# Squared scores of the first batch: columns 1 and 2 get three groups by DMA transpose in place of matmuls

## The chip, the cores and the metric

The kernel runs on one core of a Trainium2 chip. The metric is the device time of one execution in microseconds, as the median of the runs shown. Engines are called by the profile's names: PE is TensorE, DVE VectorE, ACT ScalarE, POOL GpSimd, SP SyncE.

## What is computed

Eight sequences (batches) of 3008 tokens go through a gated attention without softmax, and the result through a two-layer block. The scores are z times its own transpose, so the matrix of squared scores is symmetric, and that is what this case turns on.

```python
def _attn_ref(u, v, z):                      # u, v: (8, 3008, 256); z: (8, 3008, 64)
    scores = (1.0 / S) * np.matmul(z, z.transpose(0, 2, 1))
    attn = np.maximum(scores, 0.0) ** 2
    return u * np.matmul(attn, v)

def _moe_ref(x, w_in, w_out):                # w_in: (256, 2048), w_out: (2048, 256)
    h = x @ w_in
    return (h * np.cos(h)) @ w_out
```

## The kernel before

The 3008 tokens are 24 blocks of 128 (the last is a half), and four blocks make a group of 512. So the matrix of squared scores of a batch is 6 x 6 groups. A column c holds 512 queries, and a row R holds 512 keys; group (c,R) is a tile of 128 x 2048 half-precision numbers in one of 18 slots. Tiles that were computed have the key `a`, tiles that were turned have the key `t`.

**How a group comes about.** It is computed in two halves, called visits of pairs (`s_visit`). `s_matmuls` (L271) makes scores by matmuls that use 64 rows of the array, into four banks of PSUM. `s_squares` takes the positive part into `rt`, on ACT (L307) or, for one bank in four of the first columns, on DVE (L305), and squares it into the slot on DVE (L309). Both half visits of a first-batch group follow each other, so a group shows as four matmuls of L271. A group below the diagonal (R < c) is the transpose of group (R,c) above it. In most of the kernel it is not computed: `turn_s` (L321) issues a DMA transpose on SP from the computed slot to another one. A group on the diagonal, from column 4 of the first batch on, is computed as a triangle and filled by small transposes (L288, L293, L296).

**The first columns are an exception.** `direct(b, c, R)` is true for columns 0 to 2 of batch 0: there all six groups of a column are computed, below the diagonal too. The table `TURNS` has planned times for the transposes of the first batch; `None` means that the group is not turned.

**How a column is used.** `av_chunk` and `av_bank` (L362) multiply each block of the column with its block of v and sum in two banks (`ps_acc`). In columns 0 to 2 that is 46 products, in eight parts of up to six, with the rows in the order c, c+1, ..., so the groups below the diagonal come last. `moving` picks the tile: the computed one if there is one, otherwise the turned one. The last half block is added by `av_half` (L339). `finish` (L389) multiplies the two banks by the turned u (`ut`) and frees them; the next column's products need them. From column 4 on, part of the product is done with fewer multiplications: DVE forms sums and differences of tiles (`a_sums1` L439 and L441, `a_sums2` L451) and of v (`v_sums` L409 to L412), and PE multiplies them (`product`, L482).

**The two-layer block.** `h_quantum` makes h (L516), its cosine on ACT (L520) and the product on DVE (L523). `y_quantum` (L533) multiplies by w_out; ACT copies the result (L540). Score banks, h banks and y banks share the pool `ps_w` of six.

**What sets the order.** Each piece of work has a planned time in units, of which a column has eight; pieces are emitted in order of time, and every engine then runs its own instructions in order. PE's order is pinned. POOL issues all loads of v, u, z and the weights (L121), each held back until PE has reached a given matmul. SP issues all transposes, one after another: turned z (`turn_z`, L144), turned u (`turn_u`, L181, one `ut` for each column, from the buffers `ust0` and `ust1` in turn), groups (L321) and triangles (L296). Slots are given out ahead by `place`, from planned lifetimes (`use`): a tile goes into the slot that has been free longest. If the tile before is still being read, the writer waits.

In the profile the columns 0, 1, 2 of the first batch end near 25, 39 and 57 us, and column 3 near 81 us.

Of the kernel before, what the change touches and what calls it, by code (L numbers as in the profile page):

```python
# [14 lines left out]
def kernel(  # L15
# [31 lines left out]
    U = 8  # L47
# [184 lines left out]
    fresh = {}  # L232
    turned = {}

    def direct(b, c, R):


        return b == 0 and c <= 2

    def triangle(b, c, R):  # L240

# [2 lines left out]
    halves = {}  # L244
    slot_of = {}

    TURNS = {(0, 0, 1): None, (0, 0, 2): None, (0, 1, 2): None,
             (0, 0, 3): 1.0, (0, 0, 4): 2.4, (0, 1, 3): 7.8, (0, 0, 5): 8.0,
             (0, 2, 3): 14.4, (0, 1, 4): 14.6, (0, 2, 4): 15.8, (0, 1, 5): 20.0,
             (0, 2, 5): 22.0}  # L250
# [4 lines left out]
    def seven(b, c):  # L255

        return [] if (b, c) <= (0, NC // 2) else WSET[c]
# [20 lines left out]
    def s_squares(b, c, R, p, banks):  # L278
# [32 lines left out]
        if direct(b, c, R):  # L311
            behind(ins)
        if p == 1:
            fresh[(b, c, R)] = [t[:, :, k, :] for k in range(K)]
            if R > c and (b, c, R) not in TURNS:
                turn_s(b, c, R)

    def turn_s(b, c, R):
        tt = slot("t", b, c, R)
        turned[(b, c, R)] = tt  # L320
        nc.sync.dma_start_transpose(  # L321
            tt.rearrange("p s k w -> p (s k) w"),
            halves[(b, c, R)].rearrange("p s k w -> p (s k w)"))
# [10 lines left out]
    def av_half(b, c):  # L334

        a = fresh[(b, c, NC - 1)][K - 1]
        for nh in range(NDH):
            h = slice(nh * JLAST, (nh + 1) * JLAST)
            chain(nc.tensor.matmul(  # L339
                accs[(b, c)][nh],  # L340
                vs(b, NG - 1)[h, G - 1, nh * P:(nh + 1) * P],
                a[h], start=False, stop=False, skip_group_check=True))

    def wide(b, c):
        return min(CW, S - c * CW)

    def moving(b, c, j):
        R, k = divmod(j, K)
        if (b, c, R) in fresh:
            return CW, fresh[(b, c, R)][k]  # L350
        w = wide(b, c)
        tt = turned[(b, R, c)].rearrange("p s k w -> p s (k w)")
        return w, tt[:, k, 0:w]
# [48 lines left out]
    def v_sums(b, R):  # L402

        j = R * K
        t = vs(b, j // G)[:, j % G:j % G + K, :].rearrange("p (h k) d -> p h k d", h=2)
        o = vsum[R]
        b12, b22 = t[:, :, :, P:2 * P], t[:, 1, :, P:2 * P]
        left = t[:, 0, :, :].rearrange("p k (d w) -> p d k w", w=P)
        after(nc.vector.tensor_tensor(o[:, 0:3:2], b12, left, ALU.subtract).ins,  # L409
              before[-1], NOSYNC)  # L410
        nc.vector.tensor_tensor(o[:, 1], b22, o[:, 0], ALU.subtract)
        nc.vector.tensor_tensor(o[:, 3], t[:, 1, :, 0:P], o[:, 1], ALU.subtract)  # L412
# [24 lines left out]
    def a_sums1(b, c, R):  # L437
        s1 = quarters(b, c, R, (0, 1))
        after(nc.vector.tensor_tensor(s1, s1, quarters(b, c, R, (1, 1)), ALU.add).ins,  # L439
              before[-1], NOSYNC)  # L440
        nc.vector.tensor_tensor(  # L441
            second(b, c, R), s1, quarters(b, c, R, (0, 0)), ALU.subtract)
# [109 lines left out]
    def at(t, rank, f):  # L552
        events.append((t, rank, len(events), f))
# [9 lines left out]
    scores = []  # L563
    when = {}
    for b in range(B):
        pairs = [(b, c, R, p) for c, R in groups for p in range(2)]
        for i in range(0, len(pairs), NV):
            some = [pr for pr in pairs[i:i + NV] if not direct(*pr[:3])]
            t = b * span - lead + span * i / len(pairs)
            if some:  # L570
                scores.append((2 * math.floor(t / 2) + 1.2, some))
        for c in range(NC):
            if direct(b, c, c):
                for i in range(NC):
                    R = (c + i) % NC
                    scores.append((c * U + 4 * i / 3 - 3.1, [(b, c, R, 0), (b, c, R, 1)]))
    for t, some in scores:
        for pr in some:
            when[pr[:3]] = max(t, when.get(pr[:3], t))
# [3 lines left out]
    def use(key, first, last):  # L583
        a, z = lives.get(key, (first, last))
        lives[key] = (min(a, first), max(z, last))
# [10 lines left out]
    for t, some in scores:  # L596
        for b, c, R, p in some:
            use(("a", b, c, R), t, t + 1)
            if p == 1 and R > c and TURNS.get((b, c, R), t) is not None:
                t = TURNS.get((b, c, R), t)  # L600
                use(("t", b, c, R), t + 0.8, t + 2.5)
                use(("a", b, c, R), t, t + 3)
    for b in range(B):
        for R in range(NW):
            at(b * span + (TSUM[R] if b else 3 * U + 1 + 1.5 * R), 2, lambda b=b, R=R: v_sums(b, R))
        for c in range(NC):
            t = b * span + c * U
            W = seven(b, c)
            d = direct(b, c, c)
            ready = 1.5 + when[(b, c, NC - 1)]  # L610
            first, last = (0.6, 6.93) if d else (HALF[c] if W else 1.0, 7.3)
            room = [i for i, sc in enumerate(scores)
                    if max(ready, t + first) < sc[0] < t + last and i not in also]
            if room:
                also[min(room, key=lambda i: scores[i][0])] = lambda b=b, c=c: av_half(b, c)
            else:
                at(t + last, 3, lambda b=b, c=c: av_half(b, c))
            if d or not W:
                order = [(c + i) % NC for i in range(NC)]
            else:  # L620
                order = [R for R in range(NC) if R not in W]
            blocks = [R * K + k for R in order for k in range(K) if R * K + k < NJ - 1]
            if d:
                places = [(t + q + (0.5 if q < U - 1 else -0.05), 3) for q in range(U)]
            elif W:
                for i, R in enumerate(W):
                    at(t + SUM1[c][0] + SUM1[c][1] * i, 2, lambda b=b, c=c, R=R: a_sums1(b, c, R))
                    use(("x", b, c), t + SUM1[c][0], t + XEND)
                    use(("t", b, R, c) if R < c else ("a", b, c, R), t, t + 6.5)
                    at(t + SUM2[c][0] + SUM2[c][1] * i, 2.5, lambda b=b, c=c, R=R: a_sums2(b, c, R))  # L630
                at(t + WADD[c], 2.6, lambda b=b, c=c: keep(b, c, 0))
                at(t + RADD[c], 2.6, lambda b=b, c=c: keep(b, c, 8))
                done = [0, 0]
                for o, what in PLAN[c]:
                    for piece in what.split():
                        if piece[0] == "P":
                            n = int(piece[1])
                            at(t + o, 2, lambda b=b, c=c, n=n: product(b, c, n))
                            if n in (1, 5, 6, 7):
                                at(t + o + 0.02, 2.1, lambda b=b, c=c, n=n: keep(b, c, n))  # L640
                            continue
                        nh, size = "AB".index(piece[0]), int(piece[1:])
                        part = blocks[done[nh]:done[nh] + size]
                        done[nh] += size
                        end = done[nh] >= len(blocks)
                        at(t + o, 2, lambda b=b, c=c, nh=nh, part=part, end=end:
                           av_bank(b, c, nh, part, False, end))
                        for j in part:
                            R = j // K
                            use(("a", b, c, R) if R >= c else ("t", b, R, c), t + o, t + o + 0.3)  # L650
                assert done == [len(blocks)] * 2, (done, len(blocks))
                at(t + 7.45, 2, lambda b=b, c=c: finish(b, c))
                places = []
            else:
                places = [(t + q // 2 * 2 + (1.4 if q % 2 else 1.0), (4, 2)[q % 2])
                          for q in range(U)]
            n = 0
            for o, size in places:
                part = blocks[n:n + size]
                if part:  # L660
                    first, end = n == 0 and not W, n + size >= len(blocks)
                    at(o, 2, lambda b=b, c=c, part=part, first=first, end=end:
                       av_chunk(b, c, part, first, end))
                    for j in part:
                        R = j // K
                        use(("a", b, c, R) if R >= c or d else ("t", b, R, c), o, o + 0.3)
                n += size
            use(("a", b, c, NC - 1), t, t + last)
    place()
# [2 lines left out]
    for m in range(NT):  # L672
        b, i = divmod((m + 1) * TW - 1, S)
# [3 lines left out]
        for ts in range(NTS):  # L677
            for f4 in range(NFT // FG):
                at(th + U + 2 * ts + 0.1 + 0.2 * f4, 4,
                   lambda m=m, ts=ts, f4=f4: y_quantum(m, ts, f4))  # L680
    for key, t in TURNS.items():
        if t is not None:
            at(t, 3.5, lambda key=key: turn_s(*key))
    for b in range(B):
        t = b * span
# [73 lines left out]
```

## Time and profile before

| | |
|---|---|
| Median of 3 runs | 1214.15 us (1213.55 to 1215.6) |
| Profiled execution | 1214.96 us, span 1212.8 us |
| PE busy | 1206.3 us (99%), 8421 matmuls |
| DVE busy | 1020.1 us (84%) |
| ACT busy | 831.8 us (69%) |
| POOL busy | 145.8 us (12%) |
| SP's transposes (queue q1) | 356448 packets, 88.73 MB |
| POOL's loads (queue q0) | 100400 packets, 29.77 MB |

The page cuts the span into 40 slices of 30.3 us, with the busy share of an engine in tenths. A timeline has start and duration in us, engine, line, operation, the tiles written and read and how many instructions were merged; the brackets hold the idle time before the first of them and what ended it. For a DMA the timeline's duration is that of the issue by its queue, and the landing is told apart. Times in the text are us from the span's start.

### The profile page before, as it was taken

Reading aid. Unit: us, or ns where it says so; the run is one execution under the profiler, and the core shown is the slowest. Engines: PE = TensorE matmul, PEld = TensorE weight load, DVE = VectorE, ACT = ScalarE, POOL = GpSimd, SP = SyncE. Lnnn points to the kernel's source line nnn. Section 1 sums busy time; section 2 is a strip of 40 time slices with the busy share of each in tenths; the row PEclk is TensorE's granted clock in tenths of the full one; section 3 lists DMA queues with packets and bytes.
Section 4 is the critical chain, followed back from the end, with each engine's and each line's share of the span. In section 5 each row is a group of like instructions: output and inputs, shape, how many; then the busy total and the mean of one; then the engine's idle time right before and its main releaser. Section 6 shows DMA issues by size and latency. Waiting matters only on the chain.

```text
span 1212.8 us, 22944 instructions
## 1 busy us (share of the span) xinstructions
PE 1206.3 (99%) x8421; PEld 766.7 (63%) x8421; DVE 1020.1 (84%) x1995; ACT 831.8 (69%) x1741; POOL 145.8 (12%) x201
## 2 busy tenths in 40 slices
PE   9999999999999999999999999999999999999998
PEld 3356666666666666666666666666666666666666
DVE  7888988888888888888888888888888888888875
ACT  6767767677676777767777677776776767767555
POOL 3210101001010010100101011011110111100000
PEclk9999999999999999999999999999999999999999
DMA  9997968679586795857968579596695857956411
GB/s 147 186 168 132 148 92 131 111 120 154 103 112 113 120 155 102 129 104 113 155 103 133 101 112 161 96 133 104 109 162 94 133 104 112 159 94 120 73 33 48
DMA packets 484225, 145.02 MB, mean 120 GB/s; under 512 B 432400, under 2 KB 484112, under 8 KB 484112
## 3 DMA queue, kind: packets, MB, share of 16 engines
q1 hardware_dynamic: 356448, 88.73, 45.1%
q0 software_dynamic: 100400, 29.77, 24.9%
q10 hardware_dynamic: 27264, 25.06, 6.4%
q8 instruction: 66, 1.08, 0.4%
q14 instruction: 47, 0.39, 0.1%
HBM read 60.29 MB, written 24.64 MB: 70 GB/s over the span
## 4 chain that ended last, share of the span: by engine, by line
PE 97%; DMA 1%; issue 0%; DVE 0%; ACT 0%; POOL 0%; ACTq 0%; POOLq 0%; DVEq 0%
PE w L533 27%; PE w L516 26%; PE acc L482 19%; PE acc L362 18%; PE w L271 6%; PE acc L339 1%; DMA w_out<-in_moe_w_out_dram 1%; PE w L716 0%; ACT rt L307 0%; DVE s L309 0%; POOL zst L121 0%; PE w L222 0%; DVE x L389 0%; ACT zT L227 0%; DVE rt L305 0%
## 5 line engine op out<-in xcount | busy, mean ns | idle before, releaser
L520 ACT ACTIVATE c<-w 128x512 f16<-128x512 f32 x752 | 436.9, 619 | 258.7 <-PE w L516 210.8
L523 DVE TENSOR_TENSOR g<-w,c 128x512 f16<-128x512 f32 x752 | 492.3, 683 | 61.2 <-ACT c L520 59.5
L533 PE MATMUL w<-w_out,g 128*128 128x256 f16 x3008 | 448.6, 273 | 0.1
L516 PE MATMUL w<-x,w_in 128*128 128x512 f16 x1504 | 445.7, 379 | 0.0
L533 PEld LDWEIGHTS <-g 128*128 128x128 f16 x3008 | 294.1, 98 | 191.7 <-issue 0.8
L362 PE MATMUL acc<-s,v 128*128 128x512 f16 (+1 forms) x1024 | 290.6, 378 | 0.1
L307 ACT ACTIVATE rt<-w 128x512 f16<-128x512 f32 x489 | 253.1, 613 | 43.9 <-PE w L271 43.9
L309 DVE TENSOR_TENSOR s<-rt 128x1024 f16<-128x1024 f16 x254 | 172.7, 688 | 85.9 <-ACT rt L307 84.7
L516 PEld LDWEIGHTS <-w_in 128*128 128x128 f16 x1504 | 146.9, 98 | 73.3 <-issue 3.5
L482 PE MATMUL acc<-s,vsum 128*128 128x256 f16 (+1 forms) x1184 | 154.7, 270 | 0.0
L121 POOL DMA_DIRECT2D ust<-in_u_dram x112 | 81.2, 730 | 559.6 <-PE acc L362 534.9
L362 PEld LDWEIGHTS <-v 128*128 128x128 f16 x1024 | 95.2, 98 | 78.0 <-issue 30.6
L482 PEld LDWEIGHTS <-vsum 128*128 128x128 f16 x1184 | 114.8, 98 | 18.1 <-issue 3.0
L482 PE MATMUL acc<-s,v 128*128 128x256 f16 (+1 forms) x888 | 115.2, 270 | 0.0
L482 PEld LDWEIGHTS <-v 128*128 128x128 f16 x888 | 83.7, 98 | 19.2 <-issue 11.5
L451 DVE TENSOR_TENSOR s<-s,s 128x1024 f16<-128x1024 f16 (+1 forms) x148 | 92.8, 669 | 3.6 <-PE acc L482 3.6
L271 PE MATMUL w<-zT 64*128 64x512 f16 (+3 forms) x684 | 91.1, 362 | 1.9 <-ACT zT L227 1.1
L540 ACT ACTIVATE ob<-w 128x256 f32<-128x256 f32 x188 | 71.1, 378 | 8.6 <-PE w L533 8.4
L288 ACT ACTIVATE rt<-w 128x512 f16<-128x512 f32 (+3 forms) x176 | 62.9, 449 | 11.8 <-PE w L271 11.8
L121 POOL DMA_DIRECT2D v<-in_v_dram x40 | 31.2, 785 | 296.3 <-PE acc L482 146.5
L389 DVE TENSOR_TENSOR x<-acc,ut 128x512 f16<-128x512 f32 (+7 forms) x112 | 64.1, 596 | 2.1 <-PE acc L362 2.0
L441 DVE TENSOR_TENSOR s<-s 128x512 f16<-128x512 f16 (+1 forms) x148 | 60.0, 411 | 1.9
(37 smaller groups left out, 361.4 us busy)
## 6 DMA issues: line engine op xcount, KB each, us to landing
out_dram<-ob ACTq DMA_DIRECT2D x92, 256.0 KB, 2.4
ust<-in_u_dram POOLq DMA_DIRECT2D x80, 128.0 KB, 4.2
v<-in_v_dram POOLq DMA_DIRECT2D x16, 512.0 KB, 6.5
s<-s SPq DMA_TRANSPOSE x249, 4.4
v<-in_v_dram POOLq DMA_DIRECT2D x8, 448.0 KB, 9.4
zst<-in_z_dram POOLq DMA_DIRECT2D x14, 128.0 KB, 4.8
ust<-in_u_dram POOLq DMA_DIRECT2D x16, 96.0 KB, 5.1
w_in<-in_moe_w_in_dram POOLq DMA_DIRECT2D x4, 256.0 KB, 8.9
```

Of the source, the lines that this page charges most:

```text
L121: hold(nc.gpsimd.dma_start(dst, src))
L271: chain(nc.tensor.matmul(sp[:, s0 * P:], zt[h, R * K + k + 1 - lo, :], zt[h, j0 + s0:j0 + K, :].rearrange("p j w -> p (j w)"), start=True, ...
L307: nc.scalar.activation(rt[:, i, :], banks[k], AF.Relu)
L309: ins = nc.vector.tensor_tensor(t.rearrange("p s k w -> p k s w")[:, 2 * p:2 * p + 2], rv, rv, ALU.mult).ins
L362: chain(nc.tensor.matmul(acc[:, 0:wn], vs(b, j // G)[:, j % G, nh * P:(nh + 1) * P], a, start=(start and n == 0), stop=(last and n == len( ...
L451: after(nc.vector.tensor_tensor(dst, src, sub, ALU.subtract).ins, before[-1], NOSYNC)
L482: chain(nc.tensor.matmul(acc[bank][:, cols], lhs[:, k, :], rhs[:, k, :] if old else rhs[:, :, k * P:(k + 1) * P], start=(n in (1, 5) and i ...
L516: chain(nc.tensor.matmul(hp, w_in16[:, k, ft * P:(ft + 1) * P], x[:, k, :], start=(k == 0), stop=(k == NDH - 1)))
L520: nc.scalar.activation(c16, hp, AF.Sin, bias=math.pi / 2.0, scale=inv_s2)
L523: nc.vector.tensor_tensor(gs[(m, ft // FG)][:, ft % FG, :], hp, c16, ALU.mult)
L533: chain(nc.tensor.matmul(ys[m][:, 0:D], gs[(m, f4)][:, ft % FG, ts * P:(ts + 1) * P], w_out16[:, ft, :], start=(ft == 0), stop=(ft == NFT ...
L540: nc.scalar.activation(obs[m][:, i, :], ys[m][:, 0:D], AF.Copy, bias=0.0, scale=inv_s2)
```

## The change

Columns 1 and 2 of the first batch no longer compute the groups (1,0), (2,0) and (2,1). These are taken as DMA transposes of (0,1), (0,2) and (1,2), which were computed anyway. `direct` becomes false for the three, their scores are not emitted, their transposes get planned times in `TURNS`, and the lifetimes are registered accordingly. The condition in `moving` and in the lifetimes is rewritten to fit.

```diff
     def direct(b, c, R):
-        return b == 0 and c <= 2
+        return b == 0 and c <= 2 and (R >= c or (c, R) not in LATER)
...
-    TURNS = {(0, 0, 1): None, (0, 0, 2): None, (0, 1, 2): None,
+    LATER = ((1, 0), (2, 0), (2, 1))
+    TURNS = {(0, 0, 1): 4.6, (0, 0, 2): 8.2, (0, 1, 2): 9.6,
              (0, 0, 3): 1.0, (0, 0, 4): 2.4, (0, 1, 3): 7.8, (0, 0, 5): 8.0,
              (0, 2, 3): 14.4, (0, 1, 4): 14.6, (0, 2, 4): 15.8, (0, 1, 5): 20.0,
              (0, 2, 5): 22.0}
...
     def moving(b, c, j):
         R, k = divmod(j, K)
-        if (b, c, R) in fresh:
+        if R >= c or direct(b, c, R):
             return CW, fresh[(b, c, R)][k]
...
             if direct(b, c, c):
                 for i in range(NC):
                     R = (c + i) % NC
-                    scores.append((c * U + 4 * i / 3 - 3.1, [(b, c, R, 0), (b, c, R, 1)]))
+                    if direct(b, c, R):
+                        scores.append((c * U + 4 * i / 3 - 3.1, [(b, c, R, 0), (b, c, R, 1)]))
...
-                        use(("a", b, c, R) if R >= c or d else ("t", b, R, c), o, o + 0.3)
+                        use(("a", b, c, R) if R >= c or direct(b, c, R) else ("t", b, R, c),
+                            o, o + 0.3)
```

The change adds a line above most of the code, so a line of the kernel after is one higher (L321 becomes L322); from the planning on it is three.

## The prediction

> **What bounds the kernel now.** I read the page's slices first: TensorE (PE) is busy in every slice, and the DMA row is full in the first three, which is where the change lies.
>
> ```profile
> PE   9999999999999999999999999999999999999998
> ...
> DMA  9997968679586795857968579596695857956411
> ```
>
> Then the PE timeline of the first batch. It has no gap from 11 to 50 us: PE sets the pace, and one score visit (L271) costs PE this:
>
> ```profile
> 15.02 0.61 PE L271 MATMUL w<-zT 64*128 64x512 f16 x4
> 15.56 2.76 PE L362 MATMUL acc<-s,v 128*128 128x512 f16 x12
> 18.26 0.61 PE L271 MATMUL w<-zT 64*128 64x512 f16 x4
> 18.80 1.47 PE L362 MATMUL acc<-s,v 128*128 128x512 f16 x6
> 20.20 0.61 PE L271 MATMUL w<-zT 64*128 64x512 f16 x4
> ```
>
> Start to start, a visit and 6 products take 1.94 us, a visit and 12 take 3.24: 6 products are 1.30, so a visit with its switch is 0.64 us.
>
> Next the timeline of SP's queue, which issues every transpose (start, time to issue):
>
> ```profile
> 12.68 1.35 SPq L181 DMA_TRANSPOSE ut<-ust  x1
> ...
> 19.84 1.28 SPq L181 DMA_TRANSPOSE ut<-ust  x1
> ...
> 21.23 3.76 SPq L321 DMA_TRANSPOSE s<-s  x1
> ...
> 65.39 5.78 SPq L321 DMA_TRANSPOSE s<-s  x1
> 71.33 3.14 SPq L321 DMA_TRANSPOSE s<-s  x1
> 74.63 1.23 SPq L181 DMA_TRANSPOSE ut<-ust  x1
> ```
>
> From 19.84 to 79.75 us SP issues without a pause: one late transpose makes all behind it late. And the last of them are needed at once, as VectorE's (DVE) timeline shows: the wait in brackets is for group (3,4), issued at 65.39 and landed 9.5 us later, at 74.9.
>
> ```profile
> 74.96 0.43 DVE L439 TENSOR_TENSOR s<-s 128x512 f16<-128x512 f16 x1 [0.90 <-DMA s<-s]
> 75.30 0.75 DVE L441 TENSOR_TENSOR s<-s 128x512 f16<-128x512 f16 x2
> ...
> 76.96 2.48 DVE L523 TENSOR_TENSOR g<-w,c 128x512 f16<-128x512 f32 x4
> 81.09 0.69 DVE L389 TENSOR_TENSOR x<-acc,ut 128x512 f16<-128x512 f32 x1 [1.65 <-PE acc L362]
> ```
>
> So this chain has no slack on DMA, and DVE only 1.65 us of idle before the end of column 3.
>
> Last the DMA queues of three short windows: POOL's loads (q0) in 12 to 16.5, SP's transposes (q1) in 19.3 to 21 and in 51 to 53.
>
> ```profile
> q0 software_dynamic: 1849, 0.86, 145.9%
> ```
> ```profile
> q1 hardware_dynamic: 47, 0.01, 2.9%
> ```
> ```profile
> q1 hardware_dynamic: 2284, 0.58, 127.6%
> ```
>
> Columns: packets, MB, share. A group is 128x2048 f16, 0.524 MB, 2048 packets of 256 B; a ut is 1024. Alone, q1 moves 1142 packets a us (51 to 53): a group in 1.8 us. There is one free hole, 19.3 to 21, in which SP waited for ust1 to land (19.84).
>
> [...] next to loads, the group issued at 25.09 took 12.0 us to land. [...] the ut issued at 12.68 has no packet in 12 to 16.5, while q0 has 1849; [...] the trace's 1.8 (alone) is used. [...]
>
> **The change part by part.**
>
> *Removed on PE:* three visits, groups (1,0), (2,0), (2,1), in the order of before at 32.27, 43.17 and 46.41 us. 3 x 0.64 = 1.9 us off PE, directly on the path. *Removed on ScalarE (ACT) and DVE:* per group three L307 (1.57 us), one L305 and two L309 (about 1.9 us). No gain of its own: PE is the pace there and both run beside it.
>
> *Unchanged on PE:* the 46 products of each column; a turned tile is 512 columns wide too.
>
> *Added:* three transposes, 6144 packets, on SP. The built order puts (0,1) first of all, then ut0, then (0,2), ut1, (0,3), (0,4), (0,5), ut2, (1,2), and then the eight of before. Everything that was behind them moves, ut0 to ut3 too.
>
> *How much of it fits the hole.* (0,1)'s source is ready at 12.1 us (L309), but packets flow from 16.5 only, as they did for ut0. Before, q1 moved 2496 packets in 16.5 to 25. With a backlog the 1.7 us at 19.3 to 21 and the start-up gaps of ut1 and (0,3) fill at about 1100 a us; the loads of 22 to 25 take their part. I put the fill at 2500 packets (2000 to 3000). So the queue is 4096 - 2500 = 1600 packets late from (0,3) on, and 3650 after (1,2).
>
> *When things land then.* The loads (w_in, w_out, z, paced by PE) stay the same, so q1's running count of before serves as a clock. (0,5) is packet 12288 after; before, the count reached 12288 - 2500 = 9788 at 45.4 or so (16.5 to 45.4 holds 9626); with 1.3 us to landing, as before, 46.7 (was 41.9). (1,2), packet 15360: 51.3, landing 52 to 53.6. Late in the queue SP is the limit: an issue ends when about 1150 packets are outstanding (1040 to 1800 at the ends of the issues of 25 to 75 us), and takes 3.1 us at least. (2,5) is issued by 72.8, (3,4) 73.0 to 76.1, landing 2.0 later, as (3,5) did: 78.1. (3,5) to 79.3, ut3 79.5, landing 3.2 later: 82.7 (was 77.8).
>
> *Who waits.* The slots are placed by planned times; the actual readers are later.
> - Group (2,5) is now squared into the slot of a(0,5), whose transpose reads until 46.7. DVE would write at 42.1: it waits 4.6 us, and PE's fifth part of column 2 (48.47 before, 46.5 now) waits for it until 47.4. Loss about 1 us. Queued behind on DVE are only the four L523.
> - Group (3,3) goes into the slot of a(1,2), and PE's seventh part of column 2 reads t(1,2): DVE wants it at 50, PE at 52.7, it lands at 52 to 53.6. Behind it on DVE are three L309 and three L523 (about 4 us), which hold the 6 banks of ps_w. By 57 us PE is where it was before: the 1.9 us are gone.
> - L439 on (3,4): DVE free at 78.1 instead of 74.96, 3.1 us later. Behind it: two L441, three sums of v, four L523, done at 82.6 (79.4 before). The four banks that these free are wanted by the six L271 of 80.07; the sixth ends at 82.8 instead of 80.73. Loss 2.1 us against before, whatever PE had gained.
> - ut3 at 82.7: L389 ends at 83.4 and, for the second bank, at about 85.7. Column 4's products want these banks at 84.72 and 85.59, now 2.1 later: just hidden.
> - Next batch's zT, needed at 92.7: 88.3 before, some 91 to 92 now; hidden.
> - ut0, needed at 24.89: some 22.8 (20.2 before), as (0,1)'s 2048 packets are ahead of it; hidden, by 2 us.
> - Slots change in all later batches. No row shows that cost; between -0.5 and +1, taken as 0.2.
>
> *Sum:* the waits end on absolute times, so they are not added: +2.1 + 0.2 = **+2.3 us**. On the profiled execution, 1214.96 (its span of 1212.8 and 2.16 around it), 1217.3; it lies 0.81 above the median of 1214.15, on which the forecast is 1216.5. A change of 0.2% (2.4 us) is about what can be told from none.
>
> **Rivals.**
> - *All waits hidden:* the hole takes 4096 packets or more, (3,4) lands by 76.5, within the slack of the banks. Then the 1.9 us remain: 1212.2. For it: the hole and the start-up gaps are real, and q1 alone runs at 1142 a us. Against: in 16.5 to 21 loads share the engines, and the third group (1,2) has no hole. It decides from a fill of about 4000 on.
> - *The queue is a group later still:* with w_in's loads near (32 to 36 us: few q1 packets), a fill of 1000 makes SP issue (3,4) at 75.6 and land it at 80.7. DVE 5.8 us late, PE 4.6: 1218.8, slower. From a fill below 1500 it decides.
> - *The early part breaks:* ut0 behind (0,1) lands after 24.89, or v's last load (16.6) after its use at 20.7. Each us over stalls PE by one at 25; +1 to 2 on top, since later waits would then cover part of it.
>
> **How the numbers follow.** Main case 0.60, half of it over +2.4; hidden 0.20, of which 0.09 lies below -2.4 (DVE and ACT lighter as well); later still, with the broken start in it, 0.20. Faster 0.09, same 0.30 + 0.11 = 0.41, slower 0.30 + 0.20 = 0.50. The range takes in most of the hidden case (1212.2) and the late one up to 1 us over its centre: 1212.4 to 1219.8; the main case alone is 1214.4 to 1218.5.
>
> **What would show it.** Right: PE's parts of column 2 closer together until 46 us; SP's first L321 (the same call, a line lower in the file) at 12.1; DVE waits on DMA near 42 to 47 and 50 to 53, and a wait of 3 to 4 us at L439 near 73 to 78; L482's first products at about 86.8. Wrong: L439's wait under 1 us (the queue caught up), ut3 landing before 80, or a difference that grows after 100 us, where no group is added.

## The result, and the profile after

The kernel after takes 1223.44 us (median of 4 runs, 1222.62 to 1223.57); the kernel before, run on the same chip, takes 1214.88 us (4 runs, 1213.55 to 1217.75). The ratio is 1.0066, with an interval of 1.0046 to 1.0085: some 8 us slower. That is worse than the 1216.5 of the forecast and above the top of its range, 1219.8. Of the 97 runs of the kernel before in this case, six took more than 1217 us as well (the longest 1222.59); none of the six has a trace.

The profiled execution took 1223.57 us with a span of 1221.5, so 8.7 us of span have to be found. First the page of the kernel after: the head, the busy time of PE, and the slices.

```profile
span 1221.5 us, 22898 instructions
...
PE 1205.7 (99%) x8409; PEld 766.9 (63%) x8409; DVE 1013.9 (83%) x1986; ACT 826.5 (68%) x1732; POOL 145.9 (12%) x201
...
PE   9699999999999999999999999999999999999998
...
PEclk9899999999999999999999999999999999999999
```

Twelve matmuls are gone (8421 to 8409), which is the three visits of four. But PE is busy for only 0.6 us less, and idle for 15.8 us instead of 6.5 (span less busy). The slices say where: the second, 30.5 to 61 us, has a 6 for PE and an 8 for the clock. All others read as before.

The PE timeline of that slice shows it product by product (start and duration in us; in brackets the idle time before and what ended it):

```profile
41.05 1.46 PE L363 MATMUL acc<-s,v 128*128 128x512 f16 x6 [1.93 <-DVE x L390]
...
46.87 1.46 PE L517 MATMUL w<-x,w_in 128*128 128x512 f16 x6
55.28 2.72 PE L363 MATMUL acc<-s,v 128*128 128x512 f16 x6 [6.95 <-DVE s L310]
...
60.21 1.47 PE L363 MATMUL acc<-s,v 128*128 128x512 f16 x6
```

The last line is the same work that started at 51.84 us before: 8.4 us late. At L483's first products PE is at 92.80, before at 84.72: 8.1 us late, and it stays between 8.1 and 8.4 us late to the end. So nearly the whole loss is made once, before 61 us. It is the sum of four terms:

| term | us |
|---|---|
| three visits less | -1.9 |
| wait at 41.05 for the first bank of column 1 | +1.93 |
| stop at 48.3 to 55.3 | +6.95 |
| six products after the stop in 2.72 us instead of 1.47 | +1.25 |
| sum | +8.2 |

What PE waited for at 55.28 is a square (L310) by DVE, and DVE's own waits on DMA stand in its timeline:

```profile
39.10 1.29 DVE L310 TENSOR_TENSOR s<-rt 128x1024 f16<-128x1024 f16 x2 [2.03 <-DMA s<-s]
40.31 1.28 DVE L390 TENSOR_TENSOR x<-acc,ut 128x512 f16<-128x512 f32 x2
...
54.53 1.29 DVE L310 TENSOR_TENSOR s<-rt 128x1024 f16<-128x1024 f16 x2 [10.54 <-DMA s<-s]
...
83.77 0.42 DVE L440 TENSOR_TENSOR s<-s 128x512 f16<-128x512 f16 x1 [1.33 <-DMA s<-s]
```

The line at 54.53 is group (2,5), which writes into the slot of the computed group (0,5) and had to wait until the transpose of (0,5) had read it. The line at 39.10 is the same thing a group earlier: (2,3) waited for the slot of a(0,3), and `finish` of column 1 (40.31) stood behind it, which is PE's wait of 1.93. SP's queue shows why the transposes were late (start and time to issue; these are (0,3), (0,4), (0,5), ut2 and (1,2)):

```profile
25.06 3.56 SPq L322 DMA_TRANSPOSE s<-s  x1
28.70 10.29 SPq L322 DMA_TRANSPOSE s<-s  x1
39.09 8.85 SPq L322 DMA_TRANSPOSE s<-s  x1
48.10 2.84 SPq L181 DMA_TRANSPOSE ut<-ust  x1
51.04 3.65 SPq L322 DMA_TRANSPOSE s<-s  x1
```

The three groups landed at 39.0, 48.1 and 54.4, ut2 at 55.0, and (1,2) at 56.8. Before, (0,3), (0,4) and (0,5) had landed at 30.7, 37.1 and 41.9. So (0,5) comes 12.5 us later than before, and 7.7 later than the 46.7 of the prediction.

That the queue got slower, and not only longer, is seen in the DMA queues of 28 to 50 us (packets, MB, and the summed time of the packets as a share of 16 engines; packets that are under way at the same time count each, so that a share can pass 100%: q1 alone reads 127.1% in 55 to 57 us of the kernel after). The kernel before:

```profile
q1 hardware_dynamic: 7693, 1.93, 73.1%
q0 software_dynamic: 2614, 1.53, 63.1%
```

The kernel after:

```profile
q1 hardware_dynamic: 5200, 1.31, 80.2%
q0 software_dynamic: 2869, 1.49, 65.8%
```

POOL's loads move nearly the same bytes in this window, and they too take longer: a load of w_in lands a median of 11.2 us after its issue, before 8.9. SP's transposes move a third fewer packets, although SP always had more to give (from 25.06 to 54.69 us its issues follow each other within 0.2 us), and these packets take more time in all. A packet of q1 took 33 ns on average before (73.1% of 16 x 22 us over 7693) and 54 ns after. At its start the queue was fast: by 26 us it was 3085 packets ahead of before (6051 against 2966, counted from 16 us). By 50 us that lead was gone (11527 against 11796), with 6144 packets more to move by the size of the three groups (6240 by the two pages).

The loads were not the same at the start. In 20 to 26 us POOL's queue moved 11 packets, where it had moved 754 before, so that the transposes had this stretch for themselves. The reason is a buffer: the added (0,1) stands ahead of ut0, which landed at 23.8 us (20.2 before), and POOL can load the next u into that buffer only when ut0 has read it (POOL's timeline, before and after):

```profile
20.79 1.48 POOL L121 DMA_DIRECT2D ust<-in_u_dram  x2 [9.72 <-PE w L271]
```
```profile
24.36 1.48 POOL L121 DMA_DIRECT2D ust<-in_u_dram  x2 [12.96 <-DMA ut<-ust]
```

These two loads of 0.26 MB in all landed at 30.6 and 31.7 us (26.2 and 29.5 before), just ahead of w_in and beside (0,3). So a part of the lead at 26 us was owed.

### The profile page after: what moved, and what is told of

The parts are those of the page before. It is cut to its first block, busy times and chain, and to the rows that moved or that the text cites. A ratio compares the mean times of both kernels' runs of the same rounds, so it can differ in the third digit from the quotient of the medians.

```text
span 1221.5 us, 22898 instructions
## 1 busy us (share of the span) xinstructions
PE 1205.7 (99%) x8409; PEld 766.9 (63%) x8409; DVE 1013.9 (83%) x1986; ACT 826.5 (68%) x1732; POOL 145.9 (12%) x201
## 3 DMA queue, kind: packets, MB, share of 16 engines
q10 hardware_dynamic: 27264, 25.06, 6.5%
## 4 chain that ended last, share of the span: by engine, by line
PE 95%; DMA 2%; DVE 1%; ACT 0%; issue 0%; DVEq 0%; ACTq 0%
PE w L534 27%; PE w L517 26%; PE acc L483 18%; PE acc L363 17%; PE w L272 6%; DMA s<-s 2%; PE acc L340 1%; DVE s L310 0%; ACT rt L308 0%; PE w L719 0%; DVE g L524 0%; DVE s L452 0%; PE w L222 0%; DVE x L390 0%; DVE s L294 0%
## 5 line engine op out<-in xcount | busy, mean ns | idle before, releaser
L534 PE MATMUL w<-w_out,g 128*128 128x256 f16 x3008 | 448.6, 273 | 0.0
L534 PEld LDWEIGHTS <-g 128*128 128x128 f16 x3008 | 294.2, 98 | 191.2 <-issue 0.2
L308 ACT ACTIVATE rt<-w 128x512 f16<-128x512 f32 x480 | 248.5, 616 | 44.3 <-PE w L272 44.2
L310 DVE TENSOR_TENSOR s<-rt 128x1024 f16<-128x1024 f16 x248 | 168.7, 687 | 98.0 <-ACT rt L308 84.3
L483 PE MATMUL acc<-s,vsum 128*128 128x256 f16 (+1 forms) x1184 | 154.7, 270 | 0.2 <-DVE q L499 0.2
L483 PEld LDWEIGHTS <-vsum 128*128 128x128 f16 x1184 | 114.8, 98 | 18.5 <-issue 3.3
L483 PE MATMUL acc<-s,v 128*128 128x256 f16 (+1 forms) x888 | 115.2, 270 | 0.0
L483 PEld LDWEIGHTS <-v 128*128 128x128 f16 x888 | 83.7, 98 | 19.2 <-issue 11.5
L390 DVE TENSOR_TENSOR x<-acc,ut 128x512 f16<-128x512 f32 (+7 forms) x112 | 64.0, 595 | 1.5 <-PE acc L363 1.4
## 6 DMA issues: line engine op xcount, KB each, us to landing
w_in<-in_moe_w_in_dram POOLq DMA_DIRECT2D x4, 256.0 KB, 11.2
```

The lines of the kernel that those rows point to most:

```text
L308: nc.scalar.activation(rt[:, i, :], banks[k], AF.Relu)
L310: ins = nc.vector.tensor_tensor(t.rearrange("p s k w -> p k s w")[:, 2 * p:2 * p + 2], rv, rv, ALU.mult).ins
L483: chain(nc.tensor.matmul(acc[bank][:, cols], lhs[:, k, :], rhs[:, k, :] if old else rhs[:, :, k * P:(k + 1) * P], start=(n in (1, 5) and i ...
L534: chain(nc.tensor.matmul(ys[m][:, 0:D], gs[(m, f4)][:, ft % FG, ts * P:(ts + 1) * P], w_out16[:, ft, :], start=(ft == 0), stop=(ft == NFT ...
```

## The experiments

The question is why 6144 packets cost the queue so much more than their number, and whether the loss hangs on one wait. The theories, as the expectations number them: theory 1 is one unlucky slot (the wait of (2,5) on a(0,5)), and its rival a queue that is late as a whole, so that the stop only moves. Theory 1b is that the added packets alone are the load, theory 2 (2' for all the weights) that w_in's loads, beside which the late transposes run, slow the queue. Theory 3 is that lateness costs only where the late tile is needed, and theory 4 that what stands in the queue ahead of the next needed tile decides. In what follows "before" is always the kernel before on the same chip beside the experiment; its medians were 1214.05 us for e1 to e3, 1214.15 for e4 to e7, 1214.70 for e8 to e10 and 1214.58 for e11 to e13.

### Is it the one slot?

**e1_other_slot**: the kernel after, but group (2,5) goes into another slot.

```diff
             f = min(fit) if fit else min(free)
+            if key == ("a", 0, 2, 5):
+                f = next(g for g in fit if g[1] == 2)
```

> One change to the kernel after: the computed group (2,5) goes into the slot of (0,2), and the turned (2,4) into the one that (2,5) had, which the transpose of (0,5) reads until 54.5 us. SP's order and all transposes stay. Theory 1 (slot wait: of the 8.1 us by which the parts of column 2 fall behind, 7 are PE waiting for (2,5), which waits for that slot): the stop at 47 to 55 us goes; the next to stop PE is the turned (1,2), landed 56.8 in the kernel after, wanted at 54.7, so 2 to 4 us over before in all. Rival (the queue's lag costs the time, wherever it is felt): the stop only moves to the turned (1,2) and to L440, and 6 to 8 us over before remain.

1224.22 us, ratio 1.0069 (1.0046 to 1.0091): as slow as the kernel after. The stop at 48.3 is gone, and PE waits in its timeline at the next place instead, directly for a turned group, (1,2):

```profile
56.04 2.29 PE L363 MATMUL acc<-s,v 128*128 128x512 f16 x5 [3.81 <-DMA s<-s]
```

Later L440 waits 3.87 us, where it waited 1.33. The one slot was not the cause, only the first place where it showed.

**e1b_three_slots**: the same, and two spare slots for (2,3) and (3,3), so that all three stay clear of late readers.

```diff
-            slot_of[key] = f[1]
+            slot_of[key] = {('a', 0, 2, 3): 18, ('a', 0, 3, 3): 19}.get(key, f[1])
```

> As the run with (2,5) in another slot, and in addition (2,3) and (3,3) go into two slots of their own, which no transpose reads. Theory 1: the 1.9 us for which PE waited at 39 to 41 us (for L390, behind the square of (2,3)) are gained too, and DVE is not held at (3,3); what remains is the data wait for the turned (1,2): between -1 and +2 us against before. Rival: still 6 us or more over before, as the queue is as late as ever.

1223.44 us, ratio 1.0073 (1.0049 to 1.0097). Now PE waits 7.59 us for (1,2) alone. With the slots out of the way most of the loss stands at one data wait. The lag of the queue decides, not the places.

### What each half of the change is worth

**e2_no_transposes**: visits and transposes both left out; the products read the computed group above the diagonal in place of its transpose.

```diff
-    TURNS = {(0, 0, 1): 4.6, (0, 0, 2): 8.2, (0, 1, 2): 9.6,
+    TURNS = {(0, 0, 1): None, (0, 0, 2): None, (0, 1, 2): None,
...
-        tt = turned[(b, R, c)].rearrange("p s k w -> p s (k w)")
+        tt = (halves if b == 0 and (c, R) in LATER else turned)[(b, R, c)].rearrange("p s k w -> p s (k w)")
```

> The visits alone: the three groups are neither computed nor transposed. Columns 1 and 2 multiply (0,1), (0,2) and (1,2) as they stand, so the part of these groups in the output is not the reference's. SP's queue is as in the kernel before. All theories: 1.9 us less than before (three visits of 0.64 us); below -3 or above -1 would show that a visit is worth more or less than its time on PE.

1212.00 us, ratio 0.9982 (0.9975 to 0.9989): 2.1 us faster. The price of three visits, 1.9 us, was right.

Its queue shows one thing more. SP issues the transposes of the kernel before, in the same order, and the loads of 28 to 50 us have nearly the same bytes:

```profile
q1 hardware_dynamic: 10628, 2.67, 73.8%
q0 software_dynamic: 2615, 1.51, 61.7%
```

Yet q1 moved 10628 packets there, and 7693 in the kernel before. Here u's two loads had landed by 26.3 us and the first of w_in was issued 1.0 us earlier; whether that is the reason, no run tells. So the pace in this stretch isn't fixed by the packets and bytes of the two queues.

**e3_transposes_only**: the kernel before with all its visits, and three transposes more into a spare slot that nobody reads.

```diff
+    EXTRA = {(0, 0, 1): 4.6, (0, 0, 2): 8.2, (0, 1, 2): 9.6}
...
+    for key, t in EXTRA.items():
+        at(t, 3.5, lambda key=key: turn_more(*key))
```

> The kernel before with the three transposes added: all visits are kept, and (0,1), (0,2) and (1,2) are transposed into a spare slot that nobody reads, at the same planned times as after; (2,1) has a slot of its own. (2,5) here follows (0,3) in its slot, which lands early. Theory 1 (a slot wait needs a late transpose and a slot it still reads): no stop at 47 to 55 us; but (3,3) follows (1,3) in its slot, landed 49.2 before and some 60 us now, wanted at 52, so DVE stops there: +3 to +7 us. If the queue's lag alone is harmless: within 1 us of before. If the DMA's load itself slows PE: more than +8.

1224.83 us, ratio 1.0069 (1.0041 to 1.0096). The transposes alone, with the visits kept and other slots, lose as much as the whole change. A PE slowed by the load on the DMA, for which the expectation had more than +8, is not what the trace shows: products take 1.47 us for six until 56 us, and then PE stops for 7.94 us. The wait is again of DVE on a slot whose transpose is late, this time (3,3) on that of a(1,3) (DVE timeline):

```profile
62.26 1.90 DVE L309 TENSOR_TENSOR s<-rt 128x1024 f16<-128x1024 f16 x3 [11.18 <-DMA s<-s]
```

**e6_one_group**: only (1,0) is turned, and (2,0) and (2,1) are computed as before.

```diff
-    LATER = ((1, 0), (2, 0), (2, 1))
-    TURNS = {(0, 0, 1): 4.6, (0, 0, 2): 8.2, (0, 1, 2): 9.6,
+    LATER = ((1, 0),)
+    TURNS = {(0, 0, 1): 4.6, (0, 0, 2): None, (0, 1, 2): None,
```

> Only (1,0) is taken as a transpose of (0,1), the one that sits in the hole of SP's queue; (2,0) and (2,1) are computed as before. Theory 2: 2048 packets more, of which the hole from 16.5 to 26 us (3085 filled in the kernel after) takes nearly all, so nothing is pushed into w_in's window, and the 0.6 us of the visit remain: -1 to +0.5 us against before. If any added transpose costs by itself (a third of the loss each): +2.5 to +3.5.

1221.06 us, ratio 1.0043 (1.0027 to 1.0059). One group of 2048 packets, fewer than the 3085 by which the queue ran ahead at the start, costs some 5 us by the ratio. This was not expected. So the loss is far from proportional to the packets added. The groups that SP issued in e6 in 28 to 50 us landed a median of 12.8 us after their issue (9.3 before). What e6 has in common with the kernel after is (0,1) ahead of ut0; in the kernel after, u's load behind that ut0 was issued at 24.36 us instead of 20.79. In 28 to 50 us q1 moved 6253 packets, not far from the 5200 of the kernel after. What that place costs a version with (0,1) behind ut0 would show; none was run.

### Do order or slots help?

**e7_order_and_slots**: (1,2) goes ahead of (0,4) and (0,5) on SP, and (2,5) and (3,3) get slots of their own.

```diff
-             (0, 0, 3): 1.0, (0, 0, 4): 2.4, (0, 1, 3): 7.8, (0, 0, 5): 8.0,
+             (0, 0, 3): 1.0, (0, 0, 4): 9.7, (0, 1, 3): 7.8, (0, 0, 5): 9.8,
...
+        if (b, c, R) == (0, 1, 2):
+            first_of.append(ins)
+        elif (b, c, R) in ((0, 0, 4), (0, 0, 5)):
+            after(ins, first_of[0], NOSYNC)
```

> The kernel after with the order of SP changed: (1,2) goes ahead of (0,4) and (0,5), which nobody multiplies before 68 us; and (2,5) and (3,3) go into slots of their own, so that no tile of theirs waits for the transposes now late. The queue carries the same packets. Theory 3 (it is not the lag of the queue, but that what is late is needed: first by a slot, then by PE): no stop of PE at 39 to 58 us over 2 us, a wait at L440 near 75 to 84 us, in all -1.5 to +3 us against before. If the lag costs wherever it falls: +6 to +9.

1229.49 us, ratio 1.0126 (1.0113 to 1.0139), the worst of all. There is no stop in 47 to 58 us; the debt is paid at 70 to 91, where a load of w_out, a group's slot and a turned tile at L446 (L440 of the kernel after) are waited for in turn (PE timeline, then DVE timeline; L540 is L534 of the kernel after):

```profile
74.65 0.98 PE L540 MATMUL w<-w_out,g 128*128 128x256 f16 x4 [4.97 <-DMA w_out<-in_moe_w_out_dram]
```
```profile
79.15 0.69 DVE L310 TENSOR_TENSOR s<-rt 128x1024 f16<-128x1024 f16 x1 [11.78 <-DMA s<-s]
```

**e8_late_groups_last**: two slots more for all, the three groups of row 5 (needed only for later columns) behind ut3, and (0,4) behind (1,2).

```diff
-    NSLOT = 18
+    NSLOT = 20
...
+        if b == 0 and (c, R) in ((0, 4), (0, 5), (1, 5), (2, 5)):
+            after(ins, last_turn[0 if R == 4 else -1], NOSYNC)
```

> The kernel after with SP's order changed more: (0,5), (1,5) and (2,5), which nobody multiplies before 100 us, go behind ut3; (0,4) goes behind (1,2); two more slots hold the sources meanwhile (20 in all). Ahead of ut3 the queue has 11 groups, as many as the kernel before. Theory 4 (the loss is what stands in the queue ahead of the next needed tile): with the slow count of the kernel after, (1,2) is packet 11264, passed at 49.3 us, landing 51, wanted at 52.7; ut3 lands by 80: -2 to +2 us against before. If the mixing of loads and transposes slows the queue further as it did with (1,2) ahead of (0,4) and (0,5) (+15 there): +5 or more.

1225.06 us, ratio 1.0075 (1.0050 to 1.0099). The planner put a computed group of column 3 behind a(1,3), whose transpose was late, and DVE waited 14.01 us for it. So this run has a slot wait of its own and doesn't settle what the order alone would give. No order that was tried brought a gain.

### Is it the weights' loads?

The four loads of w_in (planned at 7, 9, 11 and 13 units) are issued by POOL at 26 to 35 us in both kernels; the last lands at 42.9 before and at 46.9 after. Those of w_out follow. Transposes run beside them in both kernels. Before, (0,3) had landed at 30.7 and (0,5) at 41.9; in the kernel after, all of (0,3), (0,4) and (0,5) pass while w_in is loaded. Theory 2 takes it that this is where the queue loses its pace.

**e4_w_in_later** and **e5_before_w_in_later**: the same edit in the kernel after and in the kernel before.

```diff
-                at(7 + 2 * q, 0, lambda q=q: load_w_in(q))
+                at(12 + 2 * q, 0, lambda q=q: load_w_in(q))
```

> The kernel after with the four loads of w_in planned 5 units later (from 12, 14, 16 and 18 in place of 7, 9, 11 and 13), so that their 1 KB packets run at 35 to 50 us instead of 31 to 45. Slots, transposes and visits as after. Theory 2 (w_in's loads starve the transposes: from 28 to 50 us the queue of SP moves 5200 packets in the kernel after, 7700 before, because three more transposes have pushed (0,4) and (0,5) into w_in's window): (0,4) and (0,5) now land by 40 instead of 48 and 54.5, PE's stop of 7 us goes; later stops may come as w_in meets (1,2): -2 to +3 us against before. Theory 1b (the added packets alone are the load; where w_in lies does not matter): +6 to +9 as after.

> The control for the last: the kernel before with w_in 5 units later. It waits for no transpose by more than 0.9 us, so all theories: within 1 us of before, unless w_in itself then lands too late for L516 (47 us on), which would show as a stop of PE there.

e4: 1224.54 us, ratio 1.0081 (1.0069 to 1.0093). (0,4) and (0,5) now are on time: 12441 packets of q1 have passed by 40 us, after 9176. The stop at 48 us is gone. But w_in then meets (1,2) and (1,3): a transpose under way in 46 to 48 us landed 17.5 us after its issue, and the waits are back at 56 and 83 us. e5: 1220.40 us, ratio 1.0048 (1.0036 to 1.0060), so that the edit costs the kernel before 6 us although no transpose was added to it; within 1 us was expected. It waits for w_out and for (3,4) at L439:

```profile
77.33 0.42 DVE L439 TENSOR_TENSOR s<-s 128x512 f16<-128x512 f16 x1 [4.23 <-DMA s<-s]
```

Moving w_in moves the transposes that come late: those that run beside it. In 44 to 50 us, when u's loads had landed, q1 moved 1042 packets in e4, against 2693 in the kernel before. The kernel before has little room either, as the 6 us of e5 show.

**e9_few_weights** and **e10_before_few_weights**: three of the four loads of w_in and of w_out are left out, and the first quarter is used for all; in the kernel after and in the kernel before.

```diff
-                hp, w_in16[:, k, ft * P:(ft + 1) * P], x[:, k, :],
+                hp, w_in16[:, k, ft % 4 * P:(ft % 4 + 1) * P], x[:, k, :],
...
-                w_out16[:, ft, :], start=(ft == 0), stop=(ft == NFT - 1)))
+                w_out16[:, ft % 4, :], start=(ft == 0), stop=(ft == NFT - 1)))
...
-            for q in range(4):
+            for q in range(1):
```

> The kernel after with three of four loads of w_in and of w_out left out (the first quarter of each stands in for all, so the two-layer block's output is not the reference's; all matmuls are issued). 1.5 MB of 3.5 MB of POOL's loads between 25 and 72 us are gone. Theory 2' (SP's queue is slow where loads run beside it[...]): the queue passes 11500 packets well before 45 us instead of 50, no stop of PE over 1 us at 47 to 58: -2.5 to 0 us against before. If the transposes are slow by themselves: +6 or more.

> The control: the kernel before with the same loads left out (and the same part of the output not the reference's). It hardly waits for DMA, so all theories: -1 to +0.5 us against before.

e9: 1213.11 us, ratio 0.9982 (0.9973 to 0.9990). e10: 1213.95 us, ratio 0.9989 (0.9980 to 0.9998). Without most of the weights' loads the change costs nothing; its median is 0.8 us below that of the control, with intervals that overlap, so that a gain isn't shown. The queues of e9 in 28 to 50 us:

```profile
q1 hardware_dynamic: 10395, 2.62, 91.7%
q0 software_dynamic: 2604, 0.97, 45.3%
```

SP's queue moves twice the packets of the kernel after, at 31 ns on average. DVE's waits on DMA in 24 to 90 us are 0.38, 0.74 and 1.48 us.

**e11_few_w_in** and **e12_few_w_out**: the kernel after with only the one of the two reduced, in the same way.

> The kernel after with three of four loads of w_in alone left out (the first quarter stands in, so the output is not the reference's); w_out as after. If w_in is what holds SP's queue from 28 to 50 us: PE's stop of 7 us goes, and -2.5 to +1 us against before. If it takes w_out, or both: +3 to +8.

> The kernel after with three of four loads of w_out alone left out (the first quarter stands in, so the output is not the reference's); w_in as after. These loads start at 46 us, behind the slow stretch of 28 to 46: if w_in is the cause, the stop at 47 to 55 stays and +6 to +9 against before; if w_out is, -2 to +2.

e11: 1214.34 us, ratio 0.9999 (0.9991 to 1.0007). e12: 1223.03 us, ratio 1.0065 (1.0051 to 1.0079). With little of w_in the stop is gone and the queue is as fast as in e9 (28 to 50 us):

```profile
q1 hardware_dynamic: 11461, 2.88, 96.1%
```

What stays in e11 are the two late waits, for w_out (2.68 us on PE, at 71.95) and at L440. With little of w_out the slot wait of (2,5) is still there (PE timeline of e12, whose profiled execution is with a span of 1216.2 us shorter than its median):

```profile
50.30 2.72 PE L363 MATMUL acc<-s,v 128*128 128x512 f16 x6 [4.28 <-DVE s L310]
```

In 28 to 50 us q1 moved 6317 packets in e12, against the 11461 of e11. So it is beside w_in that the queue becomes late, and w_out has little part in it.

**e13_w_in_burst**: the kernel after with the four loads of w_in issued one after another, in place of one every two units.

```diff
-                at(7 + 2 * q, 0, lambda q=q: load_w_in(q))
+                at(7 + 0.1 * q, 0, lambda q=q: load_w_in(q))
```

> The kernel after with all four loads of w_in one behind the other at 26 us instead of 2 units apart; everything is loaded and computed. If a load that is spread between transposes costs the queue more than its own time: the 1 MB is through by 36 us and the queue then runs alone until ust1, (0,5) lands by 45 to 48 instead of 54.5, and 0 to +4 us against before. If only the sum of packets counts: +6 to +9 as after.

1220.78 us, ratio 1.0051 (1.0038 to 1.0064), between the two forecasts. The stop is 5.34 us, and (0,5) lands at 51.2. The interval overlaps that of the kernel after (1.0046 to 1.0085), so it is not shown that bunching helps; most of the loss stays.

## Why the prediction was right or wrong, point by point

- **Visits: right.** 1.9 us were forecast, 2.1 us measured (e2).
- **The fill of the hole: right in its number, in part by luck.** 2500 packets (2000 to 3000) were forecast in 16.5 to 25 us, and 2617 came (5113 against 2496); by 26 us the lead was 3085. The forecast had the loads of 22 to 25 take their part, but these loads came only after 26 us. So the rival that the queue is a group later because the fill is only 1000 did not happen by that way, and the rival of all waits hidden, which needed about 4000, didn't either.
- **The early part: right for PE, with one reader overlooked.** ut0 landed at 23.8 (22.8 was forecast), and L390 of column 0 started at 24.88 as before. But "hidden" counted only the reader of ut0; POOL's load into the buffer that ut0 reads became 3.6 us later.
- **Where the waits are: in part right.** The slot wait of (2,5) on a(0,5) and the wait at L440 are places named. The waits for (1,2) came only where the stop at 48 us was gone (e1, e1b, e4). The wait of (2,3) on a(0,3) was missed, because no landing was worked out for (0,3): it came at 39.0 (30.7 before) and cost 1.93 us of PE, which ate the gain of the visits at 41 us already, where the forecast had it eaten by 57.
- **The step that failed: "The loads (w_in, w_out, z, paced by PE) stay the same, so q1's running count of before serves as a clock."** In 28 to 50 us the loads had nearly the same bytes (1.49 MB after, 1.53 before), but the count did not hold: q1 moved 5200 packets instead of 7693. It is not even the count of that queue beside those loads, as the 10628 of e2 show. And the loads did shift: u, which the list in the sentence leaves out, is paced by ut0, and came later. (0,5) landed at 54.4 and not at 46.7; so the term "loss about 1 us" for the slot wait measured 6.95 us, and 1.25 more for the slow products after it. With the 1.93 us above, less the visits, PE was 8.2 us late by 61 us, where the forecast had it level with before at 57 us; the 2.3 us that the forecast had for the late wait did not come on top.
- **What the runs show in its place:** e11 against e12 shows that the queue loses its pace beside w_in's loads, and e3 that the transposes alone do it, with no visit taken away. Whether it is the number of added packets or the load of u that they push ahead of w_in stays open: every version with an added transpose has both.
- **The late wait at L439/L440: wrong in its effect.** 3 to 4 us of waiting near 73 to 78 us were forecast, 1.33 came, at 83.8, and L483's first products started at 92.80 where 86.8 was forecast. An issue of a group, "3.1 us at least" in the prediction, took 1.82 us at 57.38. And PE was by then 8 us late and so was DVE: a queue that is late costs nothing more where its readers have become as late. In e1, where the early stop is smaller, the wait is 3.87.
- **The sign of the likeliest case was right, in part by luck; the size was not.** Slower had the highest chance, 0.50, but on account of the wait at L439, and the time was lost at the slot of (2,5). The range ended at 1219.8, since the rival "a group later still" was worked out with the same clock, only with another fill. A rival that doubted the clock itself was missing.

**What stays open.** Why SP's packets take 54 ns on average in 28 to 50 us, 33 ns before and 24 in e2, beside nearly the same bytes of loads, no run here tells. The late load of u alone costs nothing where little of w_in follows (e9, e11), and the queue is slow beside w_in without u next to it too (e4, 1042 packets in 44 to 50 us); beyond that its part is not shown. Spread and amount of w_in are not told apart by e13. No order with (0,1) behind ut0 was tried, nor a cleaner one than e8. Of the versions that compute all of it, none was faster than the kernel before.

## What to carry to other kernels

The running count of a DMA queue in a trace is no clock for a changed queue, not even where the other queue moves nearly the same bytes (here 5200 packets instead of 7693, beside 1.49 and 1.53 MB): when a change adds transfers ahead of a stretch that two queues share, give the pace there a range of its own, down to the slowest stretch that the trace shows. Ask also what each moved transfer frees: a transfer that lands later holds its source buffer longer, and the next load into it moves too, perhaps into a fuller stretch (ut0 landed 3.6 us later here, and u's load was issued 3.6 us later). Slots that a planner gives out by planned times are as safe as the landing of the transfers that read them; when the queue is late, mending one slot moves the stop to the next reader (e1, e1b, e7). And a gain on the busiest engine, 2 us here, is small beside what one late queue costs it, 10 us here; ask first what room the queue has.

## What the runs showed of the hardware

**The stop slowed the products that followed it.** After the stop of 6.95 us six products took 2.72 us instead of 1.47. The windows of the kernel after (length, then PE, PEld, DVE, ACT and POOL busy with counts, granted clock, DMA share, GB/s):

```profile
55.30:58.00 2.70, 2.70 (x7) 0.97 (x7) 2.32 (x4) 0.00 (x0) 0.00 (x0) 0.50 1.23 261
58.00:60.00 2.00, 1.58 (x10) 0.31 (x8) 0.69 (x1) 1.44 (x3) 0.74 (x1) 0.99 1.08 199
```

The clock is 0.50 for 2.7 us and then full again. It had been 1.00 for the first 2.9 us of the stop and 0.50 for the rest. After stops of 4.28 us (e12) and 5.34 us (e13) six products took 2.72 us too, after the wait of 1.93 us 1.46. The length of the stop doesn't settle it alone: after 3.97 us in e5 twelve products took 2.75 us as before, and after 7.94 us in e3 eight matmuls of L523 (L516 of the kernel before), which began 2.4 us after the stop had ended, still took 3.57 us instead of 1.89. What decides whether and for how long the clock falls, these runs don't show. The prediction priced no wait with it.

**Transposes beside loads moved at a fraction of their pace alone.** Those of q1 ran at 1124 packets a us alone (2248 in 55 to 57 us of the kernel after) and at 261 beside loads (784 in 43 to 46 us; before, 1483 passed in the same three microseconds, beside loads too). In 28 to 50 us the summed time of the packets of both queues went up from 136% to 146% while the bytes went down from 3.46 to 2.80 MB: the higher share went with less moved.
